# Batch 0's linear attention by head halves, with norms and x transposes by pairs of token tiles

## The chip, the cores and the metric

The kernel runs on one core of a Trainium2 chip. The metric is the device time of one execution in microseconds, as the median of three runs. Beside the timed runs there is one profiled execution, whose trace gives the durations below.

## The reference

Eight batches of eight heads, 576 tokens and 64 dimensions go through a linear attention; its output, 4608 tokens of 512 values, goes through a two-layer network with the gate h * cos(h).

```python
theta = pi/2 * arange(S) / S                      # S = 576
phi(x) = concat([relu(x) * cos(theta), relu(x) * sin(theta)])
q_p, k_p = phi(q), phi(k)                         # 128 features per head
kv  = einsum('bhsf,bhsd->bhfd', k_p, v)
z   = k_p.sum(axis=2)
num = einsum('bhsf,bhfd->bhsd', q_p, kv)
den = einsum('bhsf,bhf->bhs', q_p, z) + 1e-6
x   = (num / den)                                 # to [B*S, 512]
h   = x @ w_in                                    # 512 x 2048
out = (h * cos(h)) @ w_out                        # 2048 x 512
```

q, k, v and the weights come as float32; the kernel works in float16 with float32 accumulation, and gives float32.

## The kernel before

**Tiling.** Of a batch's 576 tokens 512 make four tiles of 128; the last 64 wait as half of a fifth tile, which two batches share. Work goes by chunks c = 0 to 8: chunk c below 8 is the 512 tokens of batch c, chunk 8 all the leftover tokens. A chunk passes attention, layer 1 (`layer1`) and layer 2 (`layer2_plain` for chunk 0, `layer2` after that). From chunk 1 on layer 2, and from chunk 3 on part of layer 1, is done by a seven-product scheme with sums of blocks on VectorE (L837, L624, L679), which saves matmuls; `w_in_sums` and `w_out_sums` prepare sums of weight blocks.

**Attention of batch 0** (`first_attention`). All of q, all of k and v in two head halves are loaded from SyncE's queue, in that order. Features: `prep` makes, for a token tile, the cosine or the sine half of the features of all heads, on VectorE (L347) or ScalarE (L346). `q_pe` transposes the q features of a tile on TensorE (L402), and VectorE or ScalarE copies them to `qT` (L408, L406). `cast_v` casts v of one tile and one head half to `V` (L361, L360). `kv` multiplies, for each head, the k features with `V` and a column of ones (L373; 40 matmuls), into two PSUM banks, one for each head half; the two halves are copied to `kvz` by ScalarE (L385) and VectorE (L387). For each token tile `num` makes numerators and denominators of all heads (L435; 8 matmuls) in a pair of banks, ATT for tiles 0 and 2, M2 for tiles 1 and 3. VectorE adds 1e-6 (L451), takes the reciprocal (L453) and multiplies (L455): this is called a norm here. Four transposes (L475) and a copy (L479) put the tile in `xT`, which layer 1 reads. Warm-up matmuls on constant data (`warm`, L945) fill TensorE while it waits: 28 first, 17 after the first q transposes, 9 between the numerators.

**Layer 1 of chunks 0 and 1** (L529). Sixteen groups of eight matmuls, each for two columns of 128 of w_in and half of the tokens, rotate over three PSUM banks M1_0 to M1_2. Each is followed by a cosine on ScalarE (L502) and a product on VectorE (L504), which frees the bank. The order is by quarters of w_in, and within a quarter by halves of the tokens, so that the second group of two already needs all four tiles.

**Layer 2 of chunk 0** (L786). Eight units of eight matmuls of 512 columns, one for each token tile and half of w_out's rows. The first four use quarters 0 and 1 of w_out; ScalarE copies their results out (L794). The other four use quarters 2 and 3, and VectorE adds them (L797). They lie between the steps of batch 1's attention (`second_attention`), which runs like that of batch 0 but for `kv`, whose one copy to `kvz` ScalarE makes (L390).

**Order of the loads.** The weights are loaded from POOL's queue. w_in's four quarters are issued after a small copy that waits for k of batch 0 (L950), quarters 0 and 1 of w_out after one that waits for w_in's first quarter (L960), quarters 2 and 3 after one that waits for q of batch 1 (L982). The loads of batch 1's k, q and v wait for a copy that reads w_in's last quarter (L975).

**Order of the work.** The functions only record steps, with engines to choose from and what each reads and writes. Two tables written out in the file, `STARTS` and `ENGS`, give each step its place and its engine; `Plan.run` sorts the steps by `STARTS` and issues them in that order, so that each engine works through its own list in order. The times in the table are only used to sort.

Of the kernel before, what the change touches and what calls it, by code (L numbers as in the profile page):

```python
# [16 lines left out]

STARTS = (
# [166 lines left out]
def kernel(  # L185
# [12 lines left out]
    P = 128  # L198
# [816 lines left out]
    def second_attention():  # L1015
        T = start[1] - 30
        for nm in ORDER1:
# [4 lines left out]
            if nm == ORDER1[HOLDW]:  # L1022
                part_of_w_out(nm, 1)
# [103 lines left out]
```

## Time and profile before

| | |
|---|---|
| Three runs | 281.62, 281.90, 282.12 us; median 281.90 us |
| Span of the profiled execution, first to last instruction | 279.7 us; the page gives no other time of this execution |
| TensorE (PE) busy | 272.6 us, 97%, 2698 matmuls |
| VectorE (DVE) busy | 236.9 us, 85% |
| ScalarE (ACT) busy | 210.2 us, 75% |
| GpSimd (POOL) busy | 82.9 us, 30% |
| DMA | 58.03 MB, mean 207 GB/s |
| Granted TensorE clock | 1.00 |

In a line of the timeline the first number is the start in us from the start of the span, the second the time that the group took; then come engine, line, operation, the tiles written and read, their shapes, and the number of instructions merged in the line. In brackets is the engine's idle time before it and what ended that. Durations overlap where an engine starts an instruction before the one ahead has ended, so that the distance from start to start is shorter than the duration. "PEld" is the load of the stationary operand, which overlaps matmuls. A table by stretch has for each stretch its length, then busy time and number of instructions of PE, PEld, DVE, ACT and POOL, the granted clock, the share of the DMA engines and GB/s.

### The profile page before, as it was taken

To read this page: it belongs to the slowest core of one execution; us is meant where nothing else is said; L and a number is where in the kernel's file an instruction comes from. 1 tells how busy PE (TensorE), PEld (TensorE's weight loads), DVE (VectorE), ACT (ScalarE), POOL (GpSimd) and SP (SyncE) were. 2 spreads that over 40 slices of the span, in tenths; PEclk is the share of its full clock that TensorE was granted. 3 is DMA by queue.
4 is the path that set the end of the run, shared out by engine and by line. 5 is a ranking of instruction groups with operands and counts; after the bars stand their busy time and mean duration, and the time that the engine had idled before them with its cause. 6 is when DMAs were issued, how large, how long until landed. Compare 5 with 4: busy or idle time off the path is not lost.

```text
span 279.7 us, 6825 instructions
## 1 busy us (share of the span) xinstructions
PE 272.6 (97%) x2698; PEld 215.5 (77%) x2698; DVE 236.9 (85%) x442; ACT 210.2 (75%) x363; POOL 82.9 (30%) x102
## 2 busy tenths in 40 slices
PE   8999999999999999999999999999999999999993
PEld 2567857787966677769777878789988888888882
DVE  1767698989999999999999998989989879873952
ACT  2756699879998897788989988995758686776330
POOL 1430020030501201520340045132534372399210
PEclk9999999999999999999999999999999999999999
DMA  6999989999999999989999998549756495698125
GB/s 207 312 202 206 340 239 241 361 301 174 335 261 271 258 249 246 234 268 259 255 258 246 242 229 284 98 115 141 163 75 139 110 156 105 152 143 123 75 77 150
DMA packets 80223, 58.03 MB, mean 207 GB/s; under 512 B 43200, under 2 KB 77248, under 8 KB 80192
## 3 DMA queue, kind: packets, MB, share of 16 engines
q1 hardware_dynamic: 68960, 39.99, 59.4%
q0 software_dynamic: 10496, 17.04, 30.1%
q10 hardware_dynamic: 736, 0.57, 0.7%
q8 instruction: 21, 0.34, 0.5%
q14 instruction: 10, 0.08, 0.1%
HBM read 36.75 MB, written 11.80 MB: 174 GB/s over the span
## 4 chain that ended last, share of the span: by engine, by line
PE 92%; ACT 3%; DVE 2%; issue 1%; POOL 0%; ACTq 0%; POOLq 0%
PE M L861 34%; PE M L667 14%; PE M L561 11%; PE M L529 9%; PE TR L667 6%; PE ATT L945 5%; PE ATT L435 3%; PE M L786 3%; PE ATT L373 3%; PE TR L561 2%; ACT KQ L346 2%; DVE x L455 1%; PE M L402 1%; PE M L373 0%; PE TR L475 0%
## 5 line engine op out<-in xcount | busy, mean ns | idle before, releaser
L861 PEld LDWEIGHTS <-gT 128*128 128x128 f16 x560 | 53.9, 98 | 8.3
L861 PE MATMUL M<-w_out_sb,gT 128*128 128x256 f16 x448 | 57.1, 273 | 0.0
L504 DVE TENSOR_TENSOR gT<-M,ch 128x512 f16<-128x512 f32 x73 | 48.5, 685 | 5.9 <-ACT ch L502 5.7
L502 ACT ACTIVATE ch<-M 128x512 f32<-128x512 f32 x75 | 43.4, 596 | 12.0 <-PE M L529 5.4
L346 ACT ACTIVATE KQ<-km,CS 128x512 f16<-128x512 f32 x57 | 38.5, 717 | 1.4 <-DMA km<-in_k_dram 1.3
L872 ACT ACTIVATE ost<-M 128x512 f32<-128x512 f32 x41 | 24.3, 596 | 17.9 <-PE M L861 13.0
L346 ACT ACTIVATE KQ<-qm,CS 128x512 f16<-128x512 f32 x46 | 31.5, 720 | 4.1 <-DMA qm<-in_q_dram 4.1
L561 PE MATMUL M<-xT,w_in_sb 128*128 128x512 f16 x136 | 33.8, 379 | 0.0
L861 PE MATMUL M<-T,S 128*128 128x256 f16 x256 | 32.4, 273 | 0.0
L667 PEld LDWEIGHTS <-w_in_sb 128*128 128x128 f16 x288 | 27.3, 98 | 4.8 <-issue 0.3
L362 POOL CAST V<-vm 128x1024 f16<-128x1024 f32 (+1 forms) x18 | 15.9, 907 | 50.8 <-DVE den L451 20.7
L529 PE MATMUL M<-xT,w_in_sb 128*128 128x256 f16 x256 | 30.3, 273 | 0.3 <-DVE gT L504 0.3
L861 PEld LDWEIGHTS <-S 128*128 128x128 f16 x256 | 24.8, 98 | 4.1 <-DVE S L837 0.2
L529 PEld LDWEIGHTS <-w_in_sb 128*128 128x128 f16 x256 | 24.4, 98 | 3.9 <-issue 0.5
L679 DVE TENSOR_TENSOR Z<-M,Z 128x512 f32<-128x512 f32 x31 | 21.1, 687 | 4.3 <-PE M L667 3.1
L561 PEld LDWEIGHTS <-w_in_sb 128*128 128x128 f16 x160 | 14.9, 98 | 12.2
L504 POOL TENSOR_TENSOR gT<-Z,ch 128x512 f16<-128x512 f32 x5 | 6.3, 1268 | 56.6 <-ACT ch L502 20.0
L455 DVE TENSOR_TENSOR x<-ATT,rec 128x512 f16<-128x512 f32 x32 | 22.1, 691 | 1.1
L435 PEld LDWEIGHTS <-qT 128*128 128x128 f16 (+1 forms) x320 | 14.8, 101 | 5.6 <-issue 3.5
L690 ACT ACTIVATE ch<-Z 128x1024 f32<-128x1024 f32 x12 | 12.7, 1057 | 6.9 <-DVE Z L679 4.8
L675 ACT ACTIVATE Z<-M 128x512 f32<-128x512 f32 x26 | 15.1, 596 | 3.4 <-PE M L667 2.4
L435 PE MATMUL ATT<-kvz,qT 128*128 128x65 f16 (+1 forms) x288 | 16.0, 195 | 0.8 <-DVE x L455 0.5
(150 smaller groups left out, 519.3 us busy)
## 6 DMA issues: line engine op xcount, KB each, us to landing
out_dram<-ost POOLq DMA_DIRECT2D x38, 256.0 KB, 4.3
qm<-in_q_dram SPq DMA_DIRECT2D x8, 640.0 KB, 6.7
km<-in_k_dram SPq DMA_DIRECT2D x8, 640.0 KB, 7.1
qm<-in_q_dram SPq DMA_DIRECT2D x8, 512.0 KB, 6.0
km<-in_k_dram SPq DMA_DIRECT2D x8, 512.0 KB, 6.0
vm<-in_v_dram SPq DMA_DIRECT2D x6, 640.0 KB, 5.7
vm<-in_v_dram SPq DMA_DIRECT2D x6, 512.0 KB, 4.6
w_in_sb<-in_moe_w_in_dram POOLq DMA_DIRECT2D x4, 512.0 KB, 8.8
```

What stands on the lines that cost most here:

```text
L346: fn = {"ACT": lambda: nc.scalar.activation(out=out_, in_=in_, func=AF.Relu, scale=sc), "DVE": lambda: nc.vector.tensor_scalar(out=out_, i ...
L362: "POOL": lambda: nc.gpsimd.tensor_copy(out=out_, in_=in_)}
L435: nc.tensor.matmul(bank[hb][ps, hh * D1:(hh + 1) * D1], lhsT=x[:, h, :], rhs=z[:, h, :], start=True, stop=True)
L455: nc.vector.tensor_tensor(out=split(x16[n][:, hs, :], k), in0=A[:, :, :, 0:D], in1=split(rec[n][:, hs], k).unsqueeze(3).broadcast_to((P, k ...
L502: act(0.5, due, lambda: nc.scalar.activation(out=ch[c], in_=bank, func=AF.Sin, bias=math.pi / 2.0, scale=1.0), [key], [("ch", c)])
L504: mul(due, 0.61, lambda q: q.tensor_tensor(out=dst, in0=bank if len(dst.shape) == 2 else bank.rearrange("p (j s) -> p j s", j=dst.shape[1] ...
L529: nc.tensor.matmul(M1[m][:, jj * 2 * P:(jj + 1) * 2 * P], lhsT=w_in_sb[:, cc, j * P:(j + 1) * P], rhs=X[:, cc, ts], start=(cc == 0), stop= ...
L561: nc.tensor.matmul(M, lhsT=w_in_sb[:, cc, j * P:(j + 1) * P], rhs=X[:, cc, :], start=(cc == 0), stop=(cc == NCT - 1))
L667: nc.tensor.matmul(bank[0][:, j * TH:(j + 1) * TH], lhsT=a(cc, j), rhs=b[:, cc, :], start=(first and j == 0 and cc == 0), stop=(last and j ...
L679: dve(0.61, due + 0.3, lambda: nc.vector.tensor_tensor(out=dst, in0=bank[0], in1=dst, op=ALU.add), [bank[1], key], [key])
L861: nc.tensor.matmul(bank[0][:, tt * MH:(tt + 1) * MH], lhsT=a[:, j, tt * P:(tt + 1) * P], rhs=b[:, j, :], start=(first and (apart or tt == ...
L872: act(0.5, due, lambda: nc.scalar.activation(out=dst, in_=view(bank), func=AF.Copy), [bank[1]], dk)
```

## The change

Batch 0's attention (`first_attention_halves`) goes by head halves after the loads and the q features, which stay as they were. For head half 0 and then 1: the k features of the half (20 half-size instructions instead of 10), the V casts of the half (3 instead of 5, two tiles at once where possible), kv of the half (`kv_half`, 20 matmuls into a bank of M2, then one copy), and then for tiles 0 and 1, and for tiles 2 and 3, `num_pair` and `x_pair`. `num_pair` makes the numerators of four heads for two tiles, one tile in each ATT bank, and one norm over both. `x_pair` transposes the two tiles' half (4 matmuls) and copies it with one instruction to `xT`, by ScalarE or VectorE. Layer 1 of chunks 0 and 1 takes two quarters of w_in for the first half of the tokens before the second half. Warm-ups are 20, 12 and 8 instead of 28, 17 and 9. In batch 1's attention the features and V casts may stand on other engines, and V casts take two tiles at once. `OPT` holds switches; those for float16 inputs, `MODE`, `H1`, `DA` and `SQ` are off, so that their branches do nothing. `STARTS` and `ENGS` are new for all steps (1375 instead of 1363): the steps of the later chunks are the same, in another order and in part on another engine.

```diff
+OPT = dict(F16=0, FAST1={3: 2, 4: 2, 5: 2, 6: 4, 7: 4, 8: 4}, MODE={}, HH='kv', LD=[['q', 3], ['k', 3], ['v',
+           0], ['v', 1]], NB=[['A0', 'A1'], ['A0', 'A1', 'M0']], XB=[['B3'], ['B3', 'M1']], W0=5, W1=6,
+           WF=[[2, 2], [2, 2]], HOLD=['k', 0], P0=1, RAW1=2, WO2=1, H1=0, DA=0, W2=0, SQ=0, NUZ=1)
...
     def layer1(c):
...
-            for quarter in range(4):
-                for hf in range(2):
+            for quarter, hf in ([(q_ + i, hf) for q_ in (0, 2) for hf in range(2) for i in range(2)] if OPT["HH"] else
+                                [(q_, hf) for q_ in range(4) for hf in range(2)]):
...
+    def kv_half(hb, bank, key, due, b=0):
+        hs = range(H)[HALVES[hb]]
...
+                for t in range(NT + 1):
+                    nc.tensor.matmul(
+                        bank[:, hh * D1:(hh + 1) * D1], lhsT=kp[:, t, h].rearrange("p g d -> p (g d)"),
+                        rhs=V1[:, t, h, :], start=(t == 0), stop=(t == NT))
...
+        copy_by_either(Z[:, hb], bank[:, 0:HB * D1], due, 0.4, 0.38, [key], [("kvz", b, hb)])
...
+    def num_pair(i, hb, due, b=0):
+        hs = HALVES[hb]
+        for t in (2 * i, 2 * i + 1):
+            bank, key = ATT[:, t % 2, :], ("ATT", t % 2)
...
+                for hh in range(HB):
+                    nc.tensor.matmul(bank[:, hh * D1:(hh + 1) * D1], lhsT=qT[t][:, hb * HB + hh, :],
+                                     rhs=kvz[b][:, hb * HB + hh, :], start=True, stop=True)
...
+        A = ATT[:, :, 0:HB * D1].rearrange("p t (h d) -> p t h d", h=HB)
...
+            nc.vector.tensor_scalar_add(out=denp[:, n], in0=A[:, :, :, D], scalar1=1e-6)
+            nc.vector.reciprocal(out=recp[:, n], in_=denp[:, n])
+            nc.vector.tensor_tensor(out=XF[:, hb, 2 * i:2 * i + 2], in0=A[:, :, :, 0:D],
+                                    in1=recp[:, n].unsqueeze(3).broadcast_to((P, 2, HB, D)), op=ALU.mult)
...
+    def x_pair(i, hb, bank, key, due, b=0):
...
+            for j in range(2):
+                x2 = XF[:, hb, 2 * i + j].rearrange("p h d -> p (h d)")
+                for c in range(NCT // 2):
+                    nc.tensor.matmul(ps[:, c, j * P:(j + 1) * P], lhsT=x2[:, c * P:(c + 1) * P], rhs=IDENT,
+                                     is_transpose=True)
...
+    def half_tiles(hb, due):
...
+                        prep(0, "k", t, g, "", due, hs)
...
+                for t, nt in ((0, 2), (2, 2), (4, 1)):
+                    cast_v(0, t, ("DVE", "ACT", "POOL"), due, hs, nt=nt)
+                kv_half(hb, *BANKS2[hb], due)
...
+            for i in range(OPT["W1"]):
+                warm(2, 0.4314, ATT[:, 1, :], [("TR", 0)] if i == 0 else [], [("ATT", 1)])
...
+            for i in range(NT // 2):
+                num_pair(i, hb, due + 2 * i)
...
+                x_pair(i, hb, *pick[kb_[i % len(kb_)]], due + 2 * i)
...
     def second_attention():
...
-                prep(1, "k", t, g, "DVE" if g == 0 else "ACT", T + 1)
+                prep(1, "k", t, g, E1 or ("DVE" if g == 0 else "ACT"), T + 1)
...
+            if OPT["HH"]:
+                for t, nt in ((0, 2), (2, 2), (4, 1)):
+                    cast_v(1, t, ("DVE", "ACT", "POOL"), T + 4 + hb, HALVES[hb], nt=nt)
+                continue
...
-    first_attention()
+    (first_attention_halves if OPT["HH"] else first_attention)()
```

More of the change, by code (lines that the diff above doesn't have):

```diff
@@ L248 @@
     NX = 4
-    den = [sb(f"den{n}", [P, H], F32) for n in range(NX)]
-    rec = [sb(f"rec{n}", [P, H], F32) for n in range(NX)]
-    x16 = [sb(f"x16_{n}", [P, H, D]) for n in range(NX)]
+    DEN, REC = [sb(n, [P, NX, H], F32) for n in ("den", "rec")]
+    den, rec = [[x[:, n] for n in range(NX)] for x in (DEN, REC)]
+    XN = sb("XN", [P, NX, H, D])
+    x16 = [XN[:, n] for n in range(NX)]
     xT = [sb(f"xT{n}", [P, NCT, SM]) for n in range(2)]
@@ L282 @@
     ORDER0, ORDER1, HOLDW, W_FIRST = "qkv", "kqv", 1, None
-    GATE1 = (w_in_sb[0:2, 0, Dff // 2 + 1:Dff // 2 + 2], [("w_in", 2)])
+    R1 = OPT["RAW1"]
+    GATE1 = ((w_in_sb[0:2, 0, R1 * Dff // 4 + 1:R1 * Dff // 4 + 2], [("w_in", R1)]) if R1 < 4 else
+             (w_out_sb[0:2, (R1 - 4) * NJT // 4, 1:2], [("w_out", R1 - 4)]))
+    HOLDW = OPT["WO2"]
     src = {"k": k, "v": v, "q": q}
@@ L344, in prep @@
         f = len(heads) / H
-        cost = {"DVE": 0.09 + 0.33 * f, "ACT": 0.12 + 0.5 * f}
+        cost = {"DVE": 0.09 + FD * f, "ACT": 0.12 + 0.5 * f}
         fn = {"ACT": lambda: nc.scalar.activation(out=out_, in_=in_, func=AF.Relu, scale=sc),
@@ L362, in cast_v @@
               "POOL": lambda: nc.gpsimd.tensor_copy(out=out_, in_=in_)}
-        either(due, {e: cost[e] for e in ([eng] if eng else VCAST)}, fn, rd, wr)
+        either(due, {e: cost[e] for e in ([eng] if isinstance(eng, str) else eng)}, fn, rd, wr)
+    full = {}
     def kv(b, due, pair=None):
@@ L398, in q_pe @@
         ps = bank.bitcast(F16).rearrange("p (h s) -> p h s", h=H)
+        more = [("qTh", t % NT, hb) for hb in range(2)] if b <= 1 and OPT["HH"] else []
         def mm():
@@ L458, in norm, with norm2 @@
                     op=ALU.mult)
-        dve(1.05 if pair is None else 1.15, due, norm, keys, [("x16", n)])
+        if OPT["DA"] and pair is None and b >= 2:
+            A, (hs, k, ks) = N[0], cut[0]
+            act(0.22, due, lambda: nc.scalar.activation(
+                out=split(den[n][:, hs], k), in_=A[:, :, :, D], func=AF.Identity, bias=EPS, scale=1.0),
+                keys, [("den", n)])
+            def norm2():
+                nc.vector.reciprocal(out=rec[n], in_=den[n])
+                nc.vector.tensor_tensor(
+                    out=split(x16[n][:, hs, :], k), in0=A[:, :, :, 0:D],
+                    in1=split(rec[n][:, hs], k).unsqueeze(3).broadcast_to((P, k, HB, D)), op=ALU.mult)
+            dve(0.87, due, norm2, keys + [("den", n)], [("x16", n)])
+            return n
+        dve(1.05 if pair is None else 1.15, due, norm, keys, [("x16", n)]
+            + ([("x16h", n, hb) for hb in range(2)] if b == 1 and OPT["HH"] else []))
         return n
@@ L577 @@
     LATE = min(c for c, nf in FAST1.items() if nf > 2)
-    assert all(FAST1[c] == NJT // 4 for c in range(LATE, NC))
     def flat(t, dt=F16):
@@ L754, in store @@
             five, four = rows(c)
-            put(due, five[:, 2 * h:2 * h + 2, :], blocks(O, n), keys, nc.gpsimd, "POOL")
-            put(due, four[:, 2 * h:2 * h + 2, :], blocks(O, 1 - n), keys, nc.gpsimd, "POOL")
+            Q = (nc.sync, "SP") if OPT["SQ"] else (nc.gpsimd, "POOL")
+            put(due, five[:, 2 * h:2 * h + 2, :], blocks(O, n), keys, *Q)
+            put(due, four[:, 2 * h:2 * h + 2, :], blocks(O, 1 - n), keys, *Q)
             return
@@ L951, in hold @@
                 out=w_in_sb[0:2, 0, :].rearrange("p (g f) -> p g f", g=4)[:, :, 0],
-                in_=raw[ORDER0[1]][0:2, 0, 0, 0:1].broadcast_to((2, 4)))
-        pl.add("POOL", 0.4, 0.5, 0, hold, hk(ORDER0[1], [0], [0]), [("w_in", g) for g in range(4)])
+                in_=raw[hn][0:2, hh, 0, 0:1].broadcast_to((2, 4)))
+        hn, hh = OPT["HOLD"] if OPT["HH"] else (ORDER0[1], 0)
+        pl.add("POOL", 0.4, 0.5, 0, hold, hk(hn, [hh], [0]), [("w_in", g) for g in range(4)])
         for g in range(4):
@@ L1013, in first_attention, with both, copy_by_either @@
             x_pe(0, t, t, *BANKS[3 - t % 2], "ACT", 8 + t, [("fill", t)])
+    def both(due, cost, fn, rd, wr, lat={"DVE": 0.13, "ACT": 0.15}):
+        pl.add([(e, cost[e], cost[e] + lat[e], fn[e]) for e in cost], 0, 0, due, None, rd, wr)
+    def copy_by_either(out_, in_, due, dc, ac, rd, wr):
+        both(due, {"DVE": dc, "ACT": ac}, {
+            "DVE": lambda: nc.vector.tensor_copy(out=out_, in_=in_),
+            "ACT": lambda: nc.scalar.activation(out=out_, in_=in_, func=AF.Copy)}, rd, wr)
@@ new lines, in q_half, with mm @@
+    def q_half(t, hb, bank, key, due):
+        hs = HALVES[hb]
+        ps = bank.bitcast(F16)[:, 0:HB * P].rearrange("p (h s) -> p h s", h=HB)
+        full[key] = False
+        def mm():
+            for hh in range(HB):
+                nc.tensor.matmul(ps[:, hh, :], lhsT=qp[:, t, hb * HB + hh].rearrange("p g d -> p (g d)"),
+                                 rhs=IDENT, is_transpose=True)
+        pe(HB, MMT, due, mm, [("qp", t, g, h) for g in range(2) for h in range(H)[hs]] + ["ID"], [key])
+        copy_by_either(qT[t][:, hs, :], ps, due, 0.4, 0.5, [key], [("qTh", t, hb)])
@@ new lines, in num_half, with mm, norm @@
+    def num_half(t, hb, bank, key, due, b=0):
+        n = t if b == 0 else xcount[0] % NX
+        full[key] = False
+        hs = HALVES[hb]
+        def mm():
+            for hh in range(HB):
+                nc.tensor.matmul(bank[:, hh * D1:(hh + 1) * D1], lhsT=qT[t][:, hb * HB + hh, :],
+                                 rhs=kvz[b][:, hb * HB + hh, :], start=True, stop=True)
+        pe(HB, MMA, due, mm, [("qTh", t, hb) if b == 0 else ("qT", t), ("kvz", b, hb)], [key])
+        A = bank[:, 0:HB * D1].rearrange("p (h d) -> p h d", h=HB)
+        def norm():
+            nc.vector.tensor_scalar_add(out=den[n][:, hs], in0=A[:, :, D], scalar1=1e-6)
+            nc.vector.reciprocal(out=rec[n][:, hs], in_=den[n][:, hs])
+            nc.vector.tensor_tensor(out=x16[n][:, hs, :], in0=A[:, :, 0:D],
+                                    in1=rec[n][:, hs].unsqueeze(2).broadcast_to((P, HB, D)), op=ALU.mult)
+        dve(0.76, due, norm, [key], [("x16h", n, hb)])
@@ new lines, in x_half, with mm @@
+    def x_half(t, hb, bank, key, due, after=(), b=0, n=None):
+        n = t if b == 0 else n
+        full[key] = False
+        cs = slice(hb * NCT // 2, (hb + 1) * NCT // 2)
+        ps = bank.bitcast(F16)[:, 0:NCT // 2 * P].rearrange("p (c s) -> p c s", c=NCT // 2)
+        x2 = x16[n].rearrange("p h d -> p (h d)")
+        def mm():
+            for i, c in enumerate(range(NCT)[cs]):
+                nc.tensor.matmul(ps[:, i, :], lhsT=x2[:, c * P:(c + 1) * P], rhs=IDENT, is_transpose=True)
+        pe(NCT // 2, MMT, due, mm, [("x16h", n, hb), "ID", *after], [key])
+        copy_by_either(xT[b][:, cs, t * P:(t + 1) * P], ps, due, 0.28, 0.36, [key] + ([("xTh", b, t)] if hb else []),
+                       [("xT", b, t) if hb else ("xTh", b, t)])
@@ new lines, in first_attention_halves @@
+    def first_attention_halves():
+        for i, nm in enumerate("kv"):
+            dve(0.53, i - 9, lambda nm=nm: nc.vector.memset(raw[nm][:, :, NT, :], 0.0), [],
+                hk(nm, ts=[NT]))
+        for i in range(OPT["W0"]):
+            warm(4, 1.293)
+        for nm, x in OPT["LD"]:
+            load(0, nm, 0, HALVES if x == 2 else (slice(0, H),) if x == 3 else (HALVES[x],))
+        weights()
+        if "q" not in OPT["HH"]:
+            for t in range(NT):
+                for g in range(2):
+                    prep(0, "q", t, g, "", t)
+                q_pe(0, t, *BANKS[t], "B", t)
+        if "k" not in OPT["HH"]:
+            for t in range(NT + 1):
+                for g in range(2):
+                    prep(0, "k", t, g, "", 4)
+        for hb in range(2):
+            half_tiles(hb, 4 + 4 * hb)
```

228 lines of the change are left out of this document (179 added, 49 removed), and 196 rows, old and new, of the table STARTS.

## The prediction

> **What bounds the kernel now.** I read the page first, then TensorE's waits, a table of busy time by stretch, and the timeline of the first 50 us.
>
> ```profile
> span 279.7 us, 6825 instructions
> PE 272.6 (97%) x2698; PEld 215.5 (77%) x2698; DVE 236.9 (85%) x442; ACT 210.2 (75%) x363; POOL 82.9 (30%) x102
> ```
>
> TensorE is the bound. What matters is when it first has real work in every slot, and where it stands still after that. Its waits in the first 60 us (sum, times, longest) are few:
>
> ```profile
> PE ATT L435 <- DVE x L455: 0.5, 1, 0.5
> PE M L529 <- DVE gT L504: 0.3, 1, 0.3
> PE ATT L435 <- ACT kvz L390: 0.2, 1, 0.2
> ```
>
> The rest of the front is filled with warm-up matmuls, so the waits alone hide what it costs. The table by stretch shows where real work is dense:
>
> ```profile
> 21.20:24.80 3.60, 3.33 (x33) 2.65 (x31) 3.22 (x9) 2.17 (x4) 0.00 (x0) 1.00 1.24 206
> 24.80:48.10 23.30, 23.05 (x251) 17.86 (x250) 19.24 (x45) 19.49 (x35) 2.39 (x7) 1.00 1.07 260
> 48.10:274.00 225.90, 225.90 (x2250) 183.84 (x2247) 202.13 (x355) 177.18 (x307) 74.28 (x81) 1.00 0.89 200
> ```
>
> The first numbers are the stretch and TensorE's busy time. From 48.10 on it is never idle (225.90 of 225.90). So the change pays exactly what it brings forward by 48.1, minus stalls that the new table puts in later. The timeline of the front:
>
> ```profile
> 18.84 0.16 DVE L451 TENSOR_SCALAR den<-ATT 128x8 f32<-128x8 f32 x1
> ...
> 20.01 0.29 PE L435 MATMUL ATT<-kvz,qT 128*128 128x65 f16 x4 [0.50 <-DVE x L455]
> ...
> 20.94 0.17 DVE L451 TENSOR_SCALAR den<-ATT 128x8 f32<-128x8 f32 x1 [0.98 <-PE ATT L435]
> ...
> 21.20 1.03 PE L529 MATMUL M<-xT,w_in_sb 128*128 128x256 f16 x8
> ...
> 23.88 10.71 PE L529 MATMUL M<-xT,w_in_sb 128*128 128x256 f16 x96 [0.27 <-DVE gT L504]
> ```
>
> A norm holds a score bank from 18.84 to 20.01 (1.17 us). The last four numerators start at 20.61, the next norm at 20.94; with 4 x 0.031 us of matmul, TensorE's result is usable 0.20 us after its slot. Layer 1 of batch 0 starts at 21.20, but its fourth group of eight matmuls only at 24.81 (23.88 + 0.87 and a short wait): from there TensorE is full. Then the loads that the middle of the front hangs on:
>
> ```profile
> 38.01 0.19 POOL L982 CAST w_out_sb<-qm 2x2 f16<-2x2 f32 x1 [11.79 <-DMA qm<-in_q_dram]
> ...
> 48.09 1.89 PE L786 MATMUL M<-w_out_sb,gT 128*128 128x512 f16 x8
> ```
>
> ```profile
> w_out_sb<-in_moe_w_out_dram POOLq DMA_DIRECT2D x1, 512.0 KB, 9.5
> ```
>
> The last quarter of w_out is issued at 39.22, after q of batch 1 has landed, and lands 9.5 us later, at 48.7. The unit of layer 2 at 48.09 is the first to need it, at its fifth matmul (48.09 + 4 x 0.216 = 48.95). That is 0.25 us of room.
>
> **The change part by part.** The order of the changed kernel's instructions is known from the built program, the durations from rows of before.
>
> Warm-ups: 54 become 40. The first 28 (9.04 us, 0.43 us each until about 7, then 0.216) become 20 and end near 8.6, before the q transposes are ready. They are off the path; worth 0.
>
> Halving k features and V casts: ten k features become twenty, ten V casts become six.
>
> ```profile
> 7.25 2.07 DVE L347 TENSOR_SCALAR KQ<-qm,CS 128x512 f16<-128x512 f32 x5 [5.27 <-DMA qm<-in_q_dram]
> ...
> 41.36 1.09 DVE L361 CAST V<-vm 128x256 f16<-128x256 f32 x5
> ```
>
> Five casts of 256 elements take 1.09 us with the last one's 0.28: 0.20 from start to start. Five features of 512 take 2.07 with the last one's 0.48: 0.40. Half the size is half the price, so halving costs 0. ScalarE's rows agree (0.31 and 0.61 from start to start). The Trainium skill, Perfetto Trace Analysis, section Optimizing Scalar/DVE Operations, speaks against halving: it gives some 60 ns of overhead to each VectorE and 93 ns to each ScalarE instruction on SBUF, whatever its size. By it, the two more instructions that ScalarE has ahead of the first kv product would cost an estimated 0.2 us; the rows show no such step, and the sum goes by the rows.
>
> The front, walked. Loads are unchanged: q features at 7.23, k at 10.52. Six q features on VectorE reach 9.6; ScalarE copies two qT (to 11.1), makes four half features (12.3) and casts V of two tiles (0.61, done 13.1). kv of half 0 runs 13.1 to 13.7 (before: first kv at 15.21). Its copy (0.2 + 0.38 + 0.1) lets the numerators start at 14.4. Before, the four norms alternate between ATT and two other banks, so that VectorE goes from one to the next; now all four pairs go through the same two ATT banks, and numerators (0.25 + 0.20) and norm (1.17) take turns: 1.62 per pair. Three pairs and one set of transposes (0.23) end at 19.5. Transposes 0.23, handover 0.20, a VectorE copy of 512 f16 (between 0.35 and 0.69, half and all of the 1024-element qT copy; I take 0.5): layer 1 starts at 20.5 instead of 21.2. Its order by token halves needs the second pair only at the fourth to fifth group, so that the fourth starts at 23.3 instead of 24.8. **Gain 1.5 us.** Bounds: 0.9 to 2.1, by 0.15 us at each of four handovers.
>
> Layer 1 of batch 0. In the new order the 13th group reuses bank M1_1 with only one other group between, and VectorE makes a w_in sum (0.60) and the 11th group's product before the 10th's. A bank's turn is handover 0.20, cosine 0.65 and product 0.75 (rows of 0.60 and 0.69, and 0.06 until the next engine starts, as from 19.95 to 20.01), 1.6 us; one group covers 0.87. **Loss 0.7 us** (0.4 to 0.8).
>
> Attention of batch 1. Its loads come out of a DMA stream that runs from 2 us on without a pause: by the last column of the table by stretch 206 GB/s between 21.2 and 24.8 us (w_in, half of w_out), 260 after. Nothing of that is moved, so q lands at 37.8 as before. On the POOL queue the hold copies now come in the order q, v, v, k, so the first k load may be issued 0.35 us later; the stream is still busy with w_out until 28, so 0 (bound +0.35). In the new order ScalarE does eight things in a row from 35.6, the first output copy of layer 2 plus 0.2: 3 x 0.61 k features, 2 x 0.49 cosines, 2 x 0.49 output copies, one 0.61 q feature, 4.4 us, and then the q feature (0.77) that TensorE waits for. Tile 1's transposes start at 40.8 (before 39.63), tile 0's copy and bank turn let tile 2 in at 42.6, kv ends at 44.4, numerators start at 45.3 (before 44.31). Three units of layer 2 are spent before 40.6, where before kept one at 40.07 as cover. Idle here: 0.2 + 0.95 + 0.1 + 0.4 = 1.65, against 0.4 + 0.1 in before. Tile 3's transposes are now ahead of that, so the fifth unit starts at 48.55 instead of 48.09. That is 1.65 - 0.5 = **1.15 us lost here.**
>
> Sum: -1.5 + 0.7 + 1.15 = +0.35 us at the fifth unit. The walk itself gives 48.55 - 48.09 = +0.46, but over before's own order it comes out 0.1 late, at 48.2; less that, the two agree.
>
> After it, the same matmuls remain in both orders (225.4 us by count). V casts of batch 1 on other engines, transposes and stores in other places: off TensorE's path, which has 4 us or more between a load's landing and its use. What the new table adds is thinner room at handovers: I find one place, near 134 us, where a copy comes 0.17 us late. Before has five such waits of 0.05 to 0.17, by the distances from start to start of its matmuls after 50 us. I take +0.1 (0 to +0.6). The tail swaps the two last row halves: 0.
>
> So the span goes from 279.7 to 280.1, and the median, 2.2 us above the profiled span, from 281.9 to **282.3 us**.
>
> **The rivals.** (1) The front's gain survives in part. For it: w_out's last quarter could land up to 1 us earlier if batch 2's first load, behind V casts in the new order, competes less; and my ScalarE walk could be too slow. Against: with an unmoved landing of 48.7 the fifth unit cannot start before 47.85, so at most 0.25 us is kept, and the walk itself is later than that. Without the bank stall (0.7) and with ScalarE's eight steps 0.6 us shorter TensorE is there at 47.2, 0.9 before 48.09: 281.0. It decides at TensorE's start of the fifth unit: before 47.6. Chance 0.17.
> (2) The new table's handovers fail after 50 us. VectorE is busy for 29.15 of the 30 us from 140 to 170; where each of six of its products there comes 0.15 us after TensorE's slot, 0.9 us more is lost: 283.2. For it: the handover of 0.20 from TensorE is barely left free in the new order. Against: the walk finds one. It decides once VectorE is late at more than five places. Chance 0.27.
> (3) TensorE's clock falls back in the front. The granted clock is full from 7 us to the end in before, with idle spells under 1 us; the new front has fewer fillers and spells up to 1 us. If it fell, about 1.6 us of front matmuls and 3.4 us of slots would double or halve: some 285. The Trainium skill, TensorE: Matmul & The Clock Gate, Part 1, lets the clock drop after an idle window of about 3.4 us; by that rule it stays. Chance 0.02.
> That the loads or the matmul count change is excluded by the built order.
>
> **How the numbers follow.** The forecast, between no change and +1 us, has 0.54. About 0.2%, 0.56 us, is what a measurement of this kernel can tell from no change. The forecast's center of +0.4 lies inside it, but near its edge: of its 0.54 I put 0.01 faster, 0.37 inside and 0.16 slower. Rival 1 puts 0.15 faster and 0.02 inside, rival 2 gives 0.26 slower and 0.01 inside, rival 3 0.02 slower. So faster 0.16, same 0.40, slower 0.44. The range takes in both rivals' prices and leaves out rival 3 and what lies beyond those prices: 280.9 to 283.4. The likeliest case's own range is 281.9 to 282.9.
>
> **What would show it.** Right: kv of half 0 near 13.1, layer 1 at 20.5, its fourth group at 23.3, a TensorE wait of 0.7 near 31.9, waits on q features and qT between 40 and 45.5, the fifth unit near 48.4, and no idle after. Wrong: a fifth unit before 47.8, w_out's last quarter landing before 48, or TensorE waits on VectorE of over 0.6 us in sum after 50.

## The result and the profile after

The changed kernel takes 284.53 us in the median of four runs (283.01 to 284.88), the kernel before 282.01 beside it: ratio 1.0077, 95% interval 1.005 to 1.0105. It is 2.5 us slower; 282.3 was forecast, within 280.9 to 283.4. The profiled execution took 284.41 us with a span of 282.6, 2.9 more than the span before.

TensorE does less work (270.9 us busy instead of 272.6, with 14 warm-up matmuls fewer) and stands still for longer. From the page, then its waits (sum, times, longest):

```profile
span 282.6 us, 6803 instructions
PE 270.9 (96%) x2684; PEld 213.8 (76%) x2684; DVE 238.6 (84%) x444; ACT 208.7 (74%) x359; POOL 82.8 (29%) x102
```

```profile
PE ATT L456 <- DMA qT<-KQ: 1.6, 2, 0.9
PE ATT L1030 <- POOL S L1014: 1.3, 1, 1.3
PE ATT L1181 <- DVE XN L1190: 1.0, 2, 0.8
PE M L1129 <- DVE V L375: 0.8, 1, 0.8
PE M L420 <- DVE qT L429: 0.8, 1, 0.8
PE M L567 <- DVE gT L541: 0.5, 1, 0.5
```

The first line is new, and it lies after 50 us, where the kernel before had no wait that its profile shows: the numerators (L456) of batch 2 wait for `qT`, which from batch 2 on is transposed by DMA. The timeline of TensorE shows where the other waits are:

```profile
13.43 0.97 PE L1129 MATMUL M<-V,KQ 128*128 128x65 f16 x20 [0.82 <-DVE V L375]
...
20.95 2.78 PE L567 MATMUL M<-xT,w_in_sb 128*128 128x256 f16 x24
23.57 0.39 PE L1203 MATMUL M<-IDENT,XN 128*128 128x128 f16 x4
23.79 8.02 PE L567 MATMUL M<-xT,w_in_sb 128*128 128x256 f16 x72
32.35 1.91 PE L567 MATMUL M<-xT,w_in_sb 128*128 128x256 f16 x16 [0.54 <-DVE gT L541]
...
43.03 0.61 PE L420 MATMUL M<-IDENT,KQ 128*128 128x128 f16 x8 [0.78 <-DVE qT L429]
...
48.86 1.89 PE L869 MATMUL M<-w_out_sb,gT 128*128 128x512 f16 x8
...
66.87 0.43 PE L456 MATMUL ATT<-kvz,qT 128*128 128x65 f16 x8 [0.86 <-DMA qT<-KQ]
...
76.91 0.43 PE L456 MATMUL ATT<-kvz,qT 128*128 128x65 f16 x8 [0.78 <-DMA qT<-KQ]
```

Layer 1 starts at 20.95 (before 21.20), its fourth group at 23.79 (24.81), and the fifth unit of layer 2 at 48.86 (48.09). From there to the end it is 282.6 - 48.86 = 233.7 us, against 279.7 - 48.09 = 231.6 before, with the same matmuls. So 0.8 us were lost by the fifth unit and 2.1 after it. The bracket counts from the end of the last matmul; from start to start, less a matmul's slot, the two waits for `qT` are 1.02 and 0.95 us, nearly all of the 2.1.

The SyncE queue explains what they wait for, before and after:

```profile
58.28 0.60 SPq L318 DMA_DIRECT2D vm<-in_v_dram  x1
59.80 6.26 SPq L412 DMA_TRANSPOSE qT<-KQ  x3
66.12 0.61 SPq L321 DMA_DIRECT2D vm<-in_v_dram  x1
66.83 1.29 SPq L412 DMA_TRANSPOSE qT<-KQ  x1
```

```profile
60.97 1.98 SPq L433 DMA_TRANSPOSE qT<-KQ  x1
63.00 0.70 SPq L335 DMA_DIRECT2D vm<-in_v_dram  x1
63.81 2.27 SPq L433 DMA_TRANSPOSE qT<-KQ  x1
66.12 1.42 SPq L332 DMA_DIRECT2D vm<-in_v_dram  x1
67.64 2.07 SPq L433 DMA_TRANSPOSE qT<-KQ  x1
69.82 0.61 SPq L332 DMA_DIRECT2D qm<-in_q_dram  x1
70.48 1.99 SPq L433 DMA_TRANSPOSE qT<-KQ  x1
```

Before, three transposes go out in a row, from 59.80, and the fourth at 66.83; after, the first goes out at 60.97, batch 3's loads stand between them and the fourth goes out at 70.48. (Batch 2's q landed at 58.51 before and at 60.10 after, and after its first ScalarE feature also stood behind a cosine that ended at 60.19.) By the completions in the trace the first landed at 66.51 before and 66.83 after, the fourth at 71.77 and 76.86. TensorE asked for the first at 67.42 before, 0.91 us after it landed. The new table has 2.6 us of matmuls less ahead of that place (three groups of layer 1 come behind it), so that TensorE was there at 65.85. The room of the four transposes, from landing to use, was 0.9, 2.1, 3.5 and 1.9 us before; after, the first and the fourth had none, and the other two 0.2 and 0.6.

### The profile page after: what moved, and what is told of

It is laid out like the page before. It is cut to its first block, busy times and chain, and to the rows that moved or that the text cites. A ratio compares the mean times of both kernels' runs of the same rounds, so it can differ in the third digit from the quotient of the medians.

```text
span 282.6 us, 6803 instructions
## 1 busy us (share of the span) xinstructions
PE 270.9 (96%) x2684; PEld 213.8 (76%) x2684; DVE 238.6 (84%) x444; ACT 208.7 (74%) x359; POOL 82.8 (29%) x102
## 4 chain that ended last, share of the span: by engine, by line
PE 88%; DMA 4%; DVE 3%; ACT 2%; issue 1%; SPq 0%; POOL 0%; POOLq 0%; DVEq 0%
PE M L944 33%; PE M L728 14%; PE M L600 10%; PE M L567 7%; PE TR L728 6%; DMA qT<-KQ 4%; PE M L869 4%; PE ATT L456 3%; PE ATT L389 3%; PE ATT L1030 2%; PE TR L600 2%; PE M L420 1%; DVE KQ L361 1%; DVE XN L1190 1%; ACT ch L539 1%; PE ATT L1181 1%
## 5 line engine op out<-in xcount | busy, mean ns | idle before, releaser
L360 ACT ACTIVATE KQ<-km,CS 128x512 f16<-128x512 f32 (+1 forms) x57 | 37.0, 687 | 1.3 <-DMA km<-in_k_dram 1.3
L477 DVE TENSOR_TENSOR XN<-ATT,rec 128x512 f16<-128x512 f32 x30 | 20.7, 692 | 1.0
L456 PEld LDWEIGHTS <-qT 128*128 128x128 f16 (+1 forms) x288 | 13.2, 101 | 6.7 <-issue 2.5
L361 DVE TENSOR_SCALAR KQ<-qm,CS 128x512 f16<-128x512 f32 x26 | 12.0, 490 | 5.8 <-DMA qm<-in_q_dram 5.8
```

The source lines that it names most:

```text
L360: fn = {"ACT": lambda: nc.scalar.activation(out=out_, in_=in_, func=AF.Relu, scale=sc), "DVE": lambda: nc.vector.tensor_scalar(out=out_, i ...
L456: nc.tensor.matmul(bank[hb][ps, hh * D1:(hh + 1) * D1], lhsT=x[:, h, :], rhs=z[:, h, :], start=True, stop=True)
L477: nc.vector.tensor_tensor(out=split(x16[n][:, hs, :], k), in0=A[:, :, :, 0:D], in1=split(rec[n][:, hs], k).unsqueeze(3).broadcast_to((P, k ...
```

## The experiments

T0 to T3 are the four transposes of batch 2's q. "Landed" is read from the completions in each trace. An edit moves steps in the table `STARTS`; the diffs show the order on the engine that results. In timed comparisons the kernel before took 281.86 to 282.27 us beside them. One profile was taken of each kernel, and it need not be of a typical run: in num_later it is the longest run (286.31 us, median 284.39), and also in front_stall, best and room_after; in sp_first, sp_num and room_k1 it is the shortest. Waits are given as in the bracket.

**Transposes first on the queue (sp_first).**

```diff
 SyncE:  T0
+        T1
+        T2
+        T3
         v of batch 3
-        T1
         v of batch 3
-        T2
         q of batch 3
-        T3
```

> The changed kernel with one edit: on SyncE's queue all four transposes of batch 2's q come before the two v loads and the first q load of batch 3. Theory A (the queue order makes the fourth transpose late): it is issued near 67.3 us instead of 70.48 and lands near 73.5 instead of 76.86, so TensorE's second wait on qT (0.78 us before 76.91) is gone, the first (0.86 before 66.87) stays: 0.95 us less, about 283.5. Theory B (batch 2's loads come too late, the queue order is no matter): no change, 284.4. Either way the v casts of batch 3 start some 4 us later, near 76 us; if that delays kv of batch 3 (80.24), part of the gain is given back.

Measured: 287.02 us, ratio 1.0169 (1.0135 to 1.0203). T3 landed at 70.47, 6 us before it was needed, as theory A had it. T0 landed at 67.52, and TensorE waited 1.7 us for it; that T1 now ran beside it isn't shown to be why, since with batch 3's loads and the stores where the changed kernel has them T0 landed anywhere from 65.90 to 67.95 (six profiles). The late v loads cost more than the transposes gave: another wait, of 1.6 us, stands before 80.6. VectorE, in its timeline:

```profile
75.55 0.69 DVE L477 TENSOR_TENSOR XN<-ATT,rec 128x512 f16<-128x512 f32 x1
78.42 0.49 DVE L361 TENSOR_SCALAR KQ<-km,CS 128x512 f16<-128x512 f32 x1 [2.18 <-POOL V L376]
78.82 0.68 DVE L541 TENSOR_TENSOR gT<-M,ch 128x512 f16<-128x512 f32 x1
79.42 0.16 DVE L473 TENSOR_SCALAR den<-ATT 128x8 f32<-128x8 f32 x1
```

The kernel lets VectorE and GpSimd steps marked `port` go only one after the other, so a k feature stood 2.18 us behind the V casts of batch 3, and the norm that TensorE needed stood behind it.

**Batch 2's k loads first (k_first).** k's buffer is free at 40.03; the first v load waits for V casts until 44.11.

```diff
 SyncE:
+        k of batch 2 (two loads)
         v of batch 2
-        k of batch 2 (two loads)
         v of batch 2
```

> The changed kernel with one edit: on SyncE's queue batch 2's two k loads come before its first v load, which waits for the last V cast of batch 1. k's buffer is free at 40.03 us, so the k loads are issued near 40.1 and 40.8 instead of 44.83 and 45.51. Theory B (late loads): q of batch 2 lands 2 us or more before 60.10, the transposes start that much earlier, both waits on qT (1.64 us) are gone: about 282.5. Theory A (the order on ScalarE and on the queue): the q features still stand behind a cosine that ends at 60.19, the first transpose is issued at 60.9 as before, and no more than 0.3 us is gained: about 284.2. W_out's last quarter, which landed at 47.54, may land 1 to 2 us later beside k; it is needed at 49.7.

Measured: 284.52 us, 1.0099 (1.0068 to 1.0131), no change. q landed at 58.66 instead of 60.10, but T0 was issued at 60.92 as theory A said, since its feature stood behind the cosine that ended at 60.28. T0 landed at 67.76 and TensorE waited 1.7 us for it; the wait for T3 was gone. W_out's last quarter landed at 49.48, 1.9 us later; in num_later, with the loads in the old order, it landed at 49.89, so this isn't the k loads' doing alone.

**The first numerators later (num_later)**, alone and **with the transposes first (sp_num)**.

```diff
 TensorE:
-        numerators of batch 2, tile 0
         layer 1 of chunk 1, two groups
+        numerators of batch 2, tile 0
         layer 1 of chunk 1, one group
```

> The changed kernel with one edit: the first numerators of batch 2 (and their norm) stand behind two of the three layer-1 groups that follow them, 1.74 us of TensorE work later; loads and transposes are unchanged. Theory A (the fourth transpose, landing at 76.86, is the hard time): the first wait (0.86) is gone, the last one grows by as much, no change: 284.4. Theory C (the new table asks for the first numerators too early, and each wait is a loss of its own): 1.0 us less, 283.4.

> The changed kernel with both edits: the four transposes of batch 2's q ahead of batch 3's loads on SyncE's queue, and the first numerators of batch 2 two layer-1 groups later. Theory A: both waits on qT are gone, 1.9 us less than the changed kernel: about 282.5, and what is left against the kernel before is the 0.8 us by which the fifth unit of layer 2 starts later. Theory B: no change from the changed kernel beyond what the later numerators give alone. Theory C: 1.0 us less, 283.4.

Measured: 284.39 (1.0078, 1.005 to 1.0105) and 288.66 (1.0244, 1.0205 to 1.0284). Alone it changes nothing, as A had it: T0 was in time, and T1 and T3 (landed at 78.76) took the wait over. Both edits together were expected at 282.5 and were the slowest of all: VectorE again stood behind the V casts, which held TensorE for 2.7 us near 81 us, and T0, landed at 68.76, was waited for 0.6 us even so.

**Loads and numerators together (k_num), the stores later (stores_late), and the kernel before with early numerators (before_num_early).**

```diff
 k_num:            k_first and num_later together
 stores_late, POOL:
-        two output stores of chunk 0
         V casts of batch 3
+        two output stores of chunk 0
 before_num_early (kernel before), TensorE:
+        numerators of batch 2, tile 0
         layer 1 of chunk 1, three groups
-        numerators of batch 2, tile 0
```

> The changed kernel with two edits: batch 2's two k loads ahead of its first v load on SyncE's queue, and the first numerators of batch 2 with their norm two layer-1 groups (1.74 us) later. With the k loads first, the first transpose landed at 67.76 and the other three 1.5 to 2.1 us before they were needed. Theory A2 (two things made the change's second loss: loads that reach SyncE's queue late, and an order that asks TensorE for the first numerators before their transpose can land; each edit alone only moves the wait): both waits on qT are under 0.3 us together, about 282.6. Theory C (the order alone): no better than the later numerators alone, 284.4. Theory L (transposes land wherever they like, 66 to 69 us for the first, by the load of the DMA engines): between 282.6 and 284.5, and the waits move about.

> The changed kernel with one edit: the two output stores of chunk 0 (each 256 KB), which POOL issues at 59.48 and 60.02, just ahead of the first transpose, are issued after batch 3's V casts, near 75 us (in the kernel before they went out at 72.9 and after). Theory S (these 0.5 MB delay the transposes; at some 300 GB/s they take 1.7 us of DMA time): the first transpose lands 1 us or more before 66.83 and the fourth before 76, the waits on qT shrink by 1 us or more, about 283.3. Theory A2 (loads and order): 0.3 us at most, 284.2.

> The kernel before with one edit: the first numerators of batch 2 and their norm stand three layer-1 groups (2.6 us of TensorE work) earlier, as far ahead as in the changed kernel. There the first transpose landed at 66.51, 0.9 us before it was needed. Theory A2: TensorE reaches them at 64.8 and waits 1.7 us for qT, and nothing later gives that back: 283.7 against 282.0. Rival (the loss after 50 us has to do with the front or with other parts of the new table): no change, 282.0.

Measured: 284.13 (1.0074, 1.0047 to 1.0101; nine runs from 282.7 to 286.3), 283.89 (1.0056, 1.0035 to 1.0078), and 283.79 (1.0061, 1.0038 to 1.0083). In k_num's profile batch 2 has no wait on `qT` and the span is 1.4 us shorter, yet its other runs are no faster than the changed kernel's: theory A2 missed by 1.5 us. There was no wait but no room either: T1 and T3 landed 0.1 us before their use. In stores_late T0 landed 3.6 us after its issue, against 5.0 to 6.8 in the six profiles with the stores ahead of it, and T1 only at 71.01, with a wait of 0.5. That fits the stores being a part, but it is one execution, and the time isn't clear of the changed kernel's. The kernel before loses what was forecast (283.7), in one wait:

```profile
PE ATT L435 <- DMA qT<-KQ: 2.0, 1, 2.0
```

Its TensorE was there at 64.92, 0.9 us earlier than in the changed kernel, so the run shows that the order alone can lose this much, not what share it has in the changed kernel.

**Without batch 3's k and v loads (no_loads3).**

```diff
     def load(b, nm, due, hs=(slice(0, H),)):
...
+            if b == 3 and nm in "kv":
+                go4 = go5 = lambda: None
```

> The changed kernel without the loads of batch 3's k and v (that batch computes with batch 1's values; 2.3 MB less to read between 56 and 72 us). Theory L (the transposes wait their turn among loads): the first transpose lands 4.5 us or less after its issue instead of 5.86, the fourth is issued before 68.5 and lands before 73; both waits on qT are gone, near 282.5. Rival (a transpose takes its 6 us by itself): landings and waits within 0.4 us of the changed kernel's.

Measured: 282.06 us, one run. The kernel leaves out 2.3 MB of loads and computes batch 3 with batch 1's k and v. The queue and, from the answer on the tile `qT` between 55 and 80 us, the time from issue to landing (no_loads3, then after):

```profile
60.76 5.18 SPq L435 DMA_TRANSPOSE qT<-KQ  x3
```

```profile
DMA to landing us min/median/max: 3.4/4.8/5.5
```

```profile
DMA to landing us min/median/max: 5.5/6.1/6.6
```

T0 landed 3.4 us after its issue instead of 5.9, and both waits are gone: 2.4 us. From the fifth unit to the end it is 231.5 us, as in the kernel before (231.6). So what the change lost there hangs on these loads beside the transposes. Two things are not told apart: how long a transpose takes beside other transfers, and the loads' own time on the queue, since the transposes now follow each other with none between.

**The front (front_stall, cover).**

```diff
 front_stall, TensorE, layer 1 of chunk 0 (columns from block 8 and 10, second half of the tokens):
-        group 10, group 8
+        group 8, group 10
 with their cosines and products; a w_in sum on VectorE two products later
 cover: front_stall, and in batch 1's attention
 ScalarE:
+        q feature of tile 1
         k feature
-        output copy
-        q feature of tile 1
         V cast, copy of qT 1, V cast
+        q feature, copy to kvz, output copy
 TensorE:
+        transposes of tile 0
         transposes of tile 1
-        transposes of tile 0
+        kv, first half
         transposes of tile 2
-        kv, first half
```

> The changed kernel with one edit: in layer 1 of chunk 0 the two groups of the third and fourth w_in quarters for the second half of the tokens change places, with their cosines and products, and a sum of w_in blocks moves two products later on VectorE, so that the wait of 0.54 us before 32.35 is gone. Theory F (what the front gains is lost again at the loads: batch 1's q lands at 37.84 and its V casts end at 44.1 whatever TensorE does before): TensorE stands 0.6 to 0.7 us longer near 40.3, numerators start at 45.5 as before, the fifth unit of layer 2 starts within 0.2 us of 48.86, and the time stays at 284.4. Rival (TensorE's own order is the path): the fifth unit starts at 48.2 and the time is 0.7 us less, 283.7.

> The changed kernel with the front alone mended: the layer-1 groups exchanged as in the run on the front's wait, and in batch 1's attention the q features of tile 1 ahead of a k feature and an output copy on ScalarE, one q feature moved to VectorE, V casts ahead of a product, tile 0 transposed ahead of tile 1, kv's first half ahead of tile 2. By my step times numerators start at 44.5 instead of 45.56 and the fifth unit at 47.9 instead of 48.86. Theory A2 (the first transpose of batch 2 cannot land before 66.5 to 68 whatever TensorE has won): the wait before the first numerators grows by nearly as much, 284.0 or over. Rival (the front's time is kept): 283.4.

Measured: 284.26 (1.0072, 1.0044 to 1.0099) and 284.03 (1.0081, 1.0054 to 1.0108). With the wait at 32.35 gone the fifth unit started at 48.46, with batch 1's attention mended too at 48.24 (47.9 was expected). The start of layer 1 moves from profile to profile, between 20.82 and 21.43; from there to the fifth unit it is 27.91 in the changed kernel (26.89 before), 27.33 in front_stall and 26.83 in cover. So 0.6 and 1.1 us were won there: theory F, which had the fifth unit unmoved, was wrong there, and cover won back all that the changed kernel loses between these two places. The time shows neither clearly: the intervals overlap the changed kernel's. In the waits of cover, T0 now takes 1.4 us, and w_out's last quarter shows:

```profile
PE ATT L456 <- DMA qT<-KQ: 1.4, 1, 1.4
...
PE M L869 <- DMA w_out_sb<-in_moe_w_out_dram: 0.3, 1, 0.3
```

**Room made (slack, best).** Both have the first numerators of batch 2 behind three layer-1 groups, the stores of chunk 0 late, and this queue; slack has k_first as well, best has cover instead.

```diff
 SyncE:  T0
+        T1
         v of batch 3
-        T1
         v of batch 3
         T2
+        T3
         q of batch 3
-        T3
```

> The changed kernel with room made for batch 2's transposes and the front left as it is: batch 2's k loads ahead of its first v load; on SyncE's queue both v loads of batch 3 between the second and third transposes and its q loads behind the fourth; the two output stores of chunk 0 after batch 3's V casts; the first numerators of batch 2 behind three layer-1 groups (2.6 us later) and the first layer-2 product of chunk 1 behind them, as the kernel before has it. Theory A2 with L (the transposes land at 65.5 to 68.8 by the load of the DMA engines, and the change left them no room): no wait on qT over 0.2 us in the profile, the spread of the runs falls to under 1.5 us, about 282.6, that is 0.4 above the kernel before, for the later fifth unit. Rival (something else of the new table): still 284.

> The front mended as in the run on batch 1's attention, and the room for batch 2's transposes as in the run on it, but with the loads of batch 2 in the changed kernel's order (k first would put w_out's last quarter past 49, where the fifth unit now needs it at 48.7). Theory A2 with L: fifth unit near 47.9, no wait on qT over 0.3 us: span near 279.7, time near 282.0, the kernel before's. Rival: a new wait near 67 or 75 us of 0.5 to 1 us, 283.

Measured: 284.80 (1.0118, 1.0083 to 1.0154) and 283.77 (1.0065, 1.0048 to 1.0082). In slack the transposes had 1.4 us and more to spare, but TensorE came to them some 2 us late; the first four matmuls of the fifth unit were followed by this:

```profile
51.90 1.02 PE L869 MATMUL M<-w_out_sb,gT 128*128 128x512 f16 x4 [1.95 <-DMA w_out_sb<-in_moe_w_out_dram]
```

The k loads, started early, ran beside w_out's last quarter, which landed at 51.85, 11.6 us after its issue (8.1 in the changed kernel). In best the fifth unit started at 47.89, as forecast, and three waits of 0.7 to 1.0 us came later: for T2, for a copy on ScalarE that stood behind a q feature of batch 3, and near 90 us for VectorE.

**The old order in the new kernel (room_after, room, room_k1, room_k4).** room_after has the queue of the kernel before (v, T0, T1, T2, v, T3, q), the numerators behind three groups and the stores late. room is that with cover, room_k1 also has one of the two k loads first, and room_k4 is room with one VectorE step moved:

```diff
 room_k4, VectorE, near 86 us:
-        k feature of batch 4
         two sums for layer 2, product of layer 1
+        k feature of batch 4
```

> The changed kernel with the stretch from 57 to 76 us put into the order of the kernel before, the front and batch 2's loads left as they are: on SyncE's queue the first v load of batch 3 ahead of the transposes, the second between the third and fourth, the q loads behind the fourth; the first numerators of batch 2 behind three layer-1 groups; the two output stores of chunk 0 after batch 3's V casts. Theory A2 with L: no wait on qT over 0.3 us, about 282.6, the 0.7 us of the later fifth unit above the kernel before. Rival D (the stream of loads from 40 to 90 us is what TensorE runs into, and each load moved back makes another late): the wait on qT is gone, but one of 0.5 us or more stands somewhere from 76 to 92 us, 283.5 or more.

> The same, with the front mended as in the run on batch 1's attention (fifth unit at 47.9 to 48.2). Theory A2: 282.0, as the kernel before. Rival D: 0.5 to 1.5 us of new waits on loads or transposes, 283 or more: what TensorE wins in front of a full stream of loads is given back.

> The same as the last, with one more edit: the first of batch 2's two k loads ahead of the first v load on SyncE's queue, issued near 40 us instead of 44, so that the stream of loads is not let run low there. Rival D: all later loads land some 1 us earlier, the waits of the last kernel shrink by as much, 282.0 or less; w_out's last quarter lands 1 us later, near 48.7, just in time. Theory A2: no change from the last kernel, or 0.3 us more for w_out.

> The kernel with the mended front and the earlier order from 57 to 76 us, with one more edit: on VectorE a k feature of batch 4, which stood waiting for its load until 86.37 us there with a product that TensorE needed queued behind it, goes behind that product. Rival D: the wait of 0.99 us before 89.78 is gone, 282.8 to 283.0; what is left over the kernel before is the waits at w_out's last quarter (0.6) and small ones from 74 to 78 us (0.6). Theory A2 (nothing there is bound to loads): no change, 283.8.

Measured: 284.34 (1.007, 1.0047 to 1.0094), 283.79 (1.0056, 1.0035 to 1.0077), 284.64 (1.0088, 1.0061 to 1.0115) and 282.77 (1.002, 1.0 to 1.004). In the first three no wait on batch 2's `qT` is left, and theory A2's 282.6 and 282.0 are missed all the same. room_after has a new wait for VectorE of 1.1 us before 90.78, as rival D had it. VectorE in room, near 86 us:

```profile
84.91 0.68 DVE L966 TENSOR_TENSOR ost<-M,ost 128x512 f32<-128x512 f32 x1
86.37 0.49 DVE L361 TENSOR_SCALAR KQ<-km,CS 128x512 f16<-128x512 f32 x1 [0.79 <-DMA km<-in_k_dram]
86.78 1.22 DVE L892 TENSOR_TENSOR T<-w_out_sb,T 128x2048 f16<-128x2048 f16 x1
87.91 1.22 DVE L981 TENSOR_TENSOR gT<-gT,S 128x2048 f16<-128x2048 f16 x1
89.05 1.28 DVE L541 TENSOR_TENSOR gT<-M,ch 128x512 f16<-128x512 f32 x2
```

A k feature waits for its load, and the product at 89.05, which frees a bank for TensorE, stands behind it: TensorE loses 0.99 us before 89.78, from start to start. With that one feature behind the product, the wait is gone and room_k4 is 1.0 us faster, as rival D said (the two intervals just overlap). room_k1 had no such wait in its profile, but 1.4 us on w_out, and its 282.0 was missed. room_k4 is 1.8 us faster than the changed kernel and equal to the kernel before within 0.4%; no version was faster than the kernel before.

## Why the prediction was wrong

**The front was walked rightly, and came out 0.4 us short**: at the fifth unit 0.77 us were lost instead of 0.35. Forecast and measured: kv of the first half at 13.1 and 13.43, layer 1 at 20.5 and 20.95, its fourth group at 23.3 and 23.79 (a gain of 1.0 instead of 1.5, within the bounds given), the bank's stall near 32 of 0.7 and 0.70 from start to start, idle in batch 1's attention of 1.65 and 1.5, the fifth unit at 48.55 and 48.86. The term that was mis-sized is the gain of 1.5, and the step behind it "halving costs 0", which compared a cast of 256 elements with a feature of 512. The walk also looked for the last V cast on ScalarE; kv waited for VectorE's (0.82 before 13.43). VectorE's work ahead of it:

```profile
10.57 2.39 DVE L361 TENSOR_SCALAR KQ<-km,CS 128x256 f16<-128x256 f32 x7
12.88 0.83 DVE L375 CAST V<-vm 128x512 f16<-128x512 f32 x2
...
14.48 0.60 DVE L361 TENSOR_SCALAR KQ<-km,CS 128x256 f16<-128x256 f32 x2
```

Seven half features took 2.31 us there (12.88 - 10.57); at half of 0.40 each they would take 1.4. Two of the seven took longer than the others, 0.43 and 0.54 from start to start. Of two in a row the first takes 0.60 - 0.34 = 0.26. ScalarE's:

```profile
10.64 1.70 ACT L360 ACTIVATE KQ<-km,CS 128x256 f16<-128x256 f32 x4
```

Four starts are (1.70 - 0.50) / 3 = 0.40 us apart, with 0.50 for the last one, not half of 0.61. That they ended at 12.3 as walked is luck: the first began at 10.64 and not at 11.1. Two halves cost some 0.12 us more than a whole on VectorE and 0.19 on ScalarE. That this made kv late fits the rows; no run tried whole features in the new order. The rule of the Trainium skill that was set aside there (Perfetto Trace Analysis, Optimizing Scalar/DVE Operations) pointed the right way: its estimate of 0.2 us for ScalarE's two more instructions stands against 0.38 by the rows (4 x 0.40 against 2 x 0.61) and 0 in the walk. The casts, measured at both sizes (0.20 and 0.33 on VectorE, 0.31 and 0.53 on ScalarE from start to start), have a fixed part of 0.07 and 0.09 us, which agrees with the 60 and 93 ns of that page of the Trainium skill.

**What failed is the sentence on everything after the fifth unit**: "off TensorE's path, which has 4 us or more between a load's landing and its use", with +0.1 us. The trace of before held the answer: T0 landed at 66.51 and was used at 67.42, 0.91 us later. That the profile shows no waits was taken for room. The sentence speaks of loads, but from batch 2 on a second transfer, the transpose, stands between a load and TensorE. Several moves of the new table went unseen together: the numerators 2.6 us of matmuls earlier, batch 3's loads between the transposes, two stores of 256 KB just ahead of them, and the first transpose itself issued 1.2 us later. In place of +0.1 the part after the fifth unit measured 2.1. The run on the kernel before (283.79) shows that early numerators alone lose 1.5 us, if they are as early as there; the run without the loads, that with them gone the waits and the 2.1 us are gone. How the 2.1 us divide among these moves stays open.

**The rivals.** None named it. The second had the right side and nearly the right size (283.2) with the wrong engine: VectorE's handovers after 50 us cost at most 0.17 us at one place. The first is wrong in its place: w_out's last quarter did land earlier, at 47.54, and was not the limit, because batch 1's attention came later. The clock's rival fell; the granted clock is 1.00 to 48 us and past it.

**What the gain of the front is worth.** front_stall and cover won 0.6 and 1.1 us up to the fifth unit, and their medians are 0.3 and 0.5 us below the changed kernel's, which the intervals don't tell from nothing. Between 40 and 90 us TensorE's order stands close behind the transfers: made earlier, it meets w_out's last quarter, the transposes, or a k load.

**What stays open.** The runs of one kernel spread by 0.9 us (front_stall) to 3.6 (k_num), those of the kernel before by 0.9 to 2.4. The spread doesn't follow the room: room_k1 and room_k4, without a wait on batch 2's `qT` in their profiles, spread by 2.7 and 2.5. What makes it isn't shown, since only one execution of each kernel was profiled. Also open is how the 0.6 us that room_k4 lacks to the kernel before are made up: of the small waits left in it, none was tried alone. The transposes' time with neither loads nor stores was not measured.

## What to carry to other kernels

An engine that is never idle in the page can still have no room: read, for each transfer that it depends on, the time between its landing and its use, before moving the use. What is issued ahead on the same queue and on others belongs to a transfer's time. When removing one wait gives nothing, look for the transfer that is next, and for the instruction that stands in an engine's queue waiting for a load while others behind it are needed; moving that one step brought 1.0 us here, more than the mended front brought in the time.

## What the runs showed of the hardware

The transposes T0 to T3, of 128 x 1024 f16 values each, took from 3.1 to 7.7 us from issue to landing in these profiles (T3 and T0 in sp_num). What makes them quick is shown only in part: T0 took 3.4 us without batch 3's k and v loads and 5.0 to 6.8 in the six profiles with these loads and the stores where the changed kernel has them. Put in a row, the second and the third landed 0.8 us apart (67.35 and 68.18 before, 67.02 and 67.86 in no_loads3). And a half-size feature has a fixed cost that a half-size cast has not to the same degree: by the two sizes some 0.12 us on VectorE and 0.19 on ScalarE for the feature, 0.07 and 0.09 for the cast.
